# Attention decode with 8 KV heads: head 6's softmax placed before a loop, c and x on another queue, fewer pieces of wo and w2

## The chip, the cores and the metric

The kernel runs on one core of a Trainium2 chip. A core has engines that run their own instruction queues: PE (TensorE, matrix multiplication; PEld is its weight load), DVE (VectorE), ACT (ScalarE), POOL (GpSimd) and SP (SyncE, which here only issues DMAs). Sixteen DMA engines move data between HBM and the on-chip memories (SBUF for data, PSUM for matmul results). The metric is the device time of one execution in microseconds, lower is better.

## The reference

One token (`x`, 512 numbers) goes through an adaptive-layernorm block: attention over a cache of 32,768 keys and values with 32 query heads that share 8 KV heads of 128 numbers, and a feed-forward layer with ReLU. Cut to what matters:

```python
mod = (_silu(c) @ w_mod).reshape(c.shape[0], 6, 1, -1)
sa, ca, ga, sb, cb, gb = (mod[:, i] for i in range(6))
h = _layernorm(x) * (1 + ca) + sa
# A: q = h @ wq (32 heads), scores = q k / sqrt(128), softmax over 32768, o = p v, then o @ wo
x = x + ga * A(h, k_cache, v_cache, wq, wo)
h = _layernorm(x) * (1 + cb) + sb
x = x + gb * (relu(h @ w1) @ w2)
```

Each of K and V is 8 x 32768 x 128 in bf16, 64 MiB, so nearly all of the 149.43 MB that the kernel reads is K and V.

## The kernel before

**The stream of loads.** All large inputs come through SyncE's DMA queue in one order, written out as a list (lines 139 to 144): w_mod, wq, K of head 0 in two halves, then for each head the halves of K of the next head and V of this one in turn, then V of head 7 in three pieces, wo in four (WOP, line 47: heads 0 to 3, 4 and 5, 6, 7), w1 in two, w2 in six (W2P, line 51). `need` (line 147) issues loads up to the one asked for. K and V halves, 4 MB each, go into a ring of five slots, so a load waits for the slot that an earlier one leaves. `c` and `x` come through GpSimd's queue (lines 156 and 157) into 16 rows of 64 numbers, eight rows each; lines 216 to 233 turn them into columns with a mask (`pick8`) and four matmuls.

**A head.** There are four K tiles per head, `u` = 0 to 3, each in two `half`s. `turn_k` (line 398) transposes one half of a tile in place on VectorE (line 405). `scores` (line 412) multiplies it with the queries: eight matmuls of 128x512 (line 422) into one PSUM bank for two tiles. `bank_max` (line 427) copies the bank to SBUF and takes each row's maximum on VectorE. `softmax` (line 433) is a generator; each `next` emits one part:

1. `m_p`, the maximum of the two halves (VectorE, line 437)
2. its transpose on TensorE (`mT_ps`, line 440)
3. `Mrow` and `Mexp` on VectorE (lines 443 and 448)
4. a transpose back on TensorE (`Mb_ps`, line 454), and on ScalarE the bias (line 456) and all exponentials (`P_g`, line 459)
5. the transposed probabilities `PT_g` (line 465) and `Lexp` (line 468) on VectorE
6. the sum over partitions on TensorE (`L_ps`, line 471)
7. its reciprocal on VectorE (`Linv`, line 474)

`pv` (line 477) multiplies the probabilities with two V tiles, 32 matmuls. For heads 0 to 5, and for the first half of head 6, it is a hardware loop in a section of its own (line 490): before its first matmul TensorE goes through a series of semaphore waits and sets the loop's registers. `blocks` (line 509) adds the four parts of a head's output on VectorE, `o_cols` (line 520) transposes it on TensorE, `normalise` (line 528) scales it and `spread` (line 544) brings a group of heads into the form that `project` (line 555) multiplies with wo.

**The order.** From line 599 the order of TensorE's and VectorE's instructions is the order in which the program emits them; an instruction that waits holds up all behind it on its engine. An iteration `g` of the loop at line 611 does the scores of head `h = g + 1` and V of head `g`, and spreads the softmax parts of head `g` over the first scores of head `h`. LAST is 7 and LOOPED is 6. At the end of iteration 5 comes part 1 of head 6's softmax, then the loop over V's second half of head 5, then part 2; iteration 6 begins with three `turn_k` of head 7 and emits parts 3 to 7 between its scores. The last iteration ends with V of head 6 and head 7, unrolled; then come `project`, the second layernorm, w1 and w2. `keep_clock` (line 592) emits matmuls whose result is not used.

Of the kernel before, what the change touches and what calls it, by code (L numbers as in the profile page):

```python
# [9 lines left out]
BF16 = mybir.dt.bfloat16  # L10
F32 = mybir.dt.float32
ACT = mybir.ActivationFunctionType
ALU = mybir.AluOpType
# [4 lines left out]
def kernel(  # L18
# [14 lines left out]
    nc = tc.nc  # L33
    P = 128
    _, _, D = A_x.shape
    _, Hkv, Sk, Dh = A_k_cache.shape
    Hq = A_wq.shape[1] // Dh
    REP = Hq // Hkv
# [8 lines left out]
    WOP = [(0, Hkv // 2), (Hkv // 2, Hkv // 4), (Hkv - 2, 1), (Hkv - 1, 1)]  # L47
    WOROWS = 2
    LAST = Hkv - 1
    LOOPED = Hkv - 2  # L50
    W2P = [(0, 4), (4, 7), (7, 10), (10, 12), (12, 13), (13, 14)]
    W1P = [(0, KT - 1), (KT - 1, KT)]
    assert Dh == 128 and REP == 4 and D == 512 and FT == W2P[-1][1] and NTILE == 4
    scale = float(Dh) ** -0.5
# [6 lines left out]
    vv = A_v_cache[0].rearrange("g (p j) d -> g p j d", p=P)  # L61
    wm_v = w_mod.rearrange("(p kt) n -> p kt n", p=P)
    wq_v = A_wq.rearrange("(p kt) n -> p kt n", p=P)
    def wo_v(i):
        g0, n = WOP[i]
        return A_wo[g0 * REP * Dh:(g0 + n) * REP * Dh, :].rearrange("(p r) d -> p r d", p=P)

    w1_v = B_w1.rearrange("(p kt) f -> p kt f", p=P)
    w2_v = B_w2.rearrange("(p f) d -> p f d", p=P)

# [4 lines left out]
    const = ctx.enter_context(tc.tile_pool(name="const", bufs=1))  # L75
# [10 lines left out]
    loaded, last_loop = {}, []  # L86
# [3 lines left out]
    def piece(name, at, n):  # L90

        if name not in pieces:
            pieces[name] = ring.tile([P, 2 * TK * Dh], BF16, tag="slot", name=name)
        return pieces[name][:, at:at + n]

    def load(key):
        kind = key[0]
        if kind == "wm":
            t = ring.tile([P, KT, 6 * D], BF16, tag="slot", name="wm_sb")
            src = wm_v  # L100
        elif kind == "wq":
            t = ring.tile([P, KT, Hq * Dh], BF16, tag="slot", name="wq_sb")
            src = wq_v
        elif kind in "kv":
            g, steps = key[1], key[2]
            src = (kv if kind == "k" else vv)[g, :, TK * steps[0]:TK * (steps[-1] + 1), :]
            name = "Ksb" if kind == "k" else "Vsb"
            if len(steps) == 2:
                t = ring.tile([P, TK * len(steps), Dh], BF16, tag="slot", name=name)
            else:  # L110
                t = piece(name, TK * Dh * (steps[0] % 2), TK * Dh).rearrange("p (j d) -> p j d", d=Dh)
        elif kind == "wo":
            g0, n = WOP[key[1]]
            t = piece("wo_sb", g0 * REP * D, n * REP * D).rearrange("p (r d) -> p r d", d=D)
            src = wo_v(key[1])
        elif kind == "w1":
            k0, k1 = W1P[key[1]]
            t = piece("w12_sb", k0 * Dff, (k1 - k0) * Dff).rearrange("p (kt f) -> p kt f", f=Dff)
            src = w1_v[:, k0:k1]
        else:  # L120
            f0, f1 = W2P[key[1]]
            t = piece("w12_sb", KT * Dff + f0 * D, (f1 - f0) * D).rearrange("p (f d) -> p f d", d=D)
            src = w2_v[:, f0:f1]
        stream_dma(t[:], src)
        if kind in "kv":
            for i, u in enumerate(steps):
                loaded[(kind, g, u)] = t[:, TK * i:TK * (i + 1), :]
        else:
            loaded[key] = t[:]

    def stream_dma(dst, src):
        i = nc.sync.dma_start(out=dst, in_=src)
        tc.stamp_issue_order_token(i.ins, "sp_stream")
        if last_loop:

            tc.add_manual_dep(i.ins, last_loop[0], mybir.DependencyInfo(
                mybir.DependencyClass.NoSync, mybir.DependencyReason.DATA))

    stream = [("wm",), ("wq",)] + [("k", 0, (2 * G, 2 * G + 1)) for G in range(NG)]
    for g in range(LAST):  # L140
        for G in range(NG):
            stream += [(kind, gg, (2 * G, 2 * G + 1)) for kind, gg in (("k", g + 1), ("v", g))]
    stream += [("v", LAST, (0, 1)), ("v", LAST, (2,)), ("v", LAST, (3,))] + [("wo", i) for i in range(len(WOP))]
    stream += [("w1", i) for i in range(len(W1P))] + [("w2", i) for i in range(len(W2P))]
    pos = [0]

# [5 lines left out]


    wm_sb = need(("wm",))
    cx_row = const.tile([16, D // 8], BF16)
    nc.gpsimd.dma_start(out=cx_row[0:8], in_=c[0].rearrange("(a n) -> a n", a=8))
    nc.gpsimd.dma_start(out=cx_row[8:16], in_=A_x[0, 0].rearrange("(a n) -> a n", a=8))

    ident_bf = const.tile([P, P], BF16)
    make_identity(nc, ident_bf[:])  # L160
# [8 lines left out]
    for hp in range(4):  # L169
        h, par = hp // 2, hp % 2  # L170
        src = AP(ib.tensor, ib.offset + 64 * h + par, [[ib.ap[0][0], P], [0, 4], [2, 32]])
# [8 lines left out]
        out=mask4, in_=ident_f[:].rearrange("p (x q) -> p q x", q=REP), op=ALU.add, axis=AX.X,  # L180
# [3 lines left out]
    for n in sorted({n * REP for _, n in WOP}):  # L184
# [28 lines left out]
    hid_bd = const.tile([P, FT, KT, KT], BF16)  # L213
    nc.gpsimd.memset(hid_bd[:], 0.0)

    pick8 = const.tile([16, 8], BF16)
    nc.vector.tensor_tensor(out=pick8[:], in0=ident_bf[0:16, 0:8], in1=ident_bf[0:16, 8:16], op=ALU.add)
    cx_sel = const.tile([16, 2], BF16)
    nc.vector.tensor_copy(out=cx_sel[:], in_=cmask[8][0:16, 0:2])
    cx_bd = const.tile([16, 8, D // 8], BF16)  # L220
    nc.vector.tensor_tensor(  # L221
        out=cx_bd[:], in0=cx_row[:].unsqueeze(1).to_broadcast([16, 8, D // 8]),
        in1=pick8[:].unsqueeze(2).to_broadcast([16, 8, D // 8]), op=ALU.mult,
    )
    xc_ps = small_ps([P, KT, 2], "xc_ps")
    for kt in range(KT):
# [171 lines left out]
    def turn_k(g, u, half):  # L398

        if u == 0 and half == 0:  # L400
            S_tiles[g] = spool.tile([P, NG, 512], F32, tag="S_g", name="S_g")
            m_tiles[g] = spool.tile([P, NG], F32, tag="m2", name="m2")
        Ksb = need(("k", g, u))
        KTt = Ksb[:, 32 * half:32 * half + 32, :].rearrange("p j d -> p (j d)")
        t = nc.vector.transpose(out=KTt.bitcast(F32), in_=KTt.bitcast(F32))  # L405
        KT_tiles[g, u, half] = KTt
        if loop:

            tc.add_manual_dep(t.ins, loop.pop(), mybir.DependencyInfo(
                mybir.DependencyClass.NoSync, mybir.DependencyReason.DATA))  # L410

    def scores(g, u, half):

        t4 = (2 * u + half) % 4
        if t4 == 0:
            S_ps_tiles[g] = bank("S_ps")
        KTv = KT_tiles.pop((g, u, half)).rearrange("p (jj h i par) -> p jj h i par", jj=32, h=2, i=32, par=2)
        for sl in range(2):
            s = 2 * t4 + sl
            for hp in range(4):  # L420
                h, par = hp // 2, hp % 2
                nc.tensor.matmul(  # L422
                    S_ps_tiles[g], lhsT=qbd[g % 2][:, hp, 4 * (7 - s):4 * (7 - s) + P], rhs=KTv[:, 16 * sl:16 * sl + 16, h, :, par],
                    start=(t4 == 0 and sl == 0 and hp == 0), stop=(t4 == 3 and sl == 1 and hp == 3),
                )
# [94 lines left out]
    def o_cols(g):  # L520
        nc.tensor.matmul(  # L521
            oT_ps, lhsT=Y_tiles.pop(g)[:], rhs=qsel, start=True, stop=True, skip_group_check=True,
        )
# [75 lines left out]
    with tc.manual_schedule(engines={mybir.EngineType.PE, mybir.EngineType.DVE}):  # L599
# [11 lines left out]
        for g in range(LAST):  # L611
            h = g + 1
            build_qbd(h)
            turn_k(h, 0, 0)
            turn_k(h, 0, 1)
            turn_k(h, 1, 0)
            scores(h, 0, 0)
            if soft:
                next(soft)
            open_o(g)  # L620
            scores(h, 0, 1)
            if soft:
                next(soft)
            if g > 0:
                blocks(g - 1)
            scores(h, 1, 0)
            if g > 0:
                o_cols(g - 1)
            turn_k(h, 1, 1)
            scores(h, 1, 1)  # L630
            if soft:
                next(soft)
            if g > 0:
                normalise(g - 1)
                if g in [sum(w) for w in WOP]:
                    spread(part_of(g - 1))
            if soft:
                next(soft)
            bank_max(h, 0)
            next(soft or iter(()), None)  # L640
            pv(g, (0, 1))
            for u in (2, 3):
                for half in range(2):
                    turn_k(h, u, half)
                    scores(h, u, half)
            bank_max(h, 1)
            soft = softmax(h)
            next(soft)
            if g < LOOPED:
                pv(g, (2, 3))  # L650
                next(soft)
                continue
            next(soft)
            next(soft)
            pv(g, (2,), range(6))
            next(soft)
            next(soft)
            open_o(LAST)
            pv(g, (2,), range(6, 16))
            pv(g, (3,))  # L660
            next(soft)
            next(soft, None)
            a_rows.append(row_bank("a_ps"))
            blocks(g)
# [109 lines left out]
```

## Time and profile before

| | before |
|---|---|
| median of 3 runs | 355.39 us (355.18 to 355.49) |
| the profiled execution's own time | 355.74 us |
| its span, from the first to the last instruction | 353.9 us |
| PE busy | 279.8 us (79%) |
| DVE busy | 203.1 us (57%) |
| ACT busy | 25.4 us (7%) |
| read from HBM | 149.42 MB, 422 GB/s over the span |
| mean granted TensorE clock | 0.947 |

The profile gives every instruction of one execution with its start, its length and what released it from a wait; times are counted from the first instruction. "L422" is line 422 of the kernel. In the page's slices the span is cut into 40 equal parts, and a digit is a share in tenths. A timeline row has the start, the duration, the engine, the line, the operation, output `<-` inputs, how many instructions were merged, and in brackets how long the engine stood idle before it and what ended that. A row of a table by stretches has, for each engine, busy microseconds and the number of instructions, then the granted clock of TensorE (1.00 is full), the busy share of the DMA engines and the rate.

### The profile page before, as it was taken

What the parts mean: (1) busy time and instruction counts of PE and PEld (TensorE: products, weight loads), DVE (VectorE), ACT (ScalarE), POOL (GpSimd) and SP (SyncE); (2) the same over time, 40 slices, a digit from 0 to 9 for tenths busy, and PEclk for the clock granted to TensorE, in tenths of its full rate; (3) what the DMA queues carried; (4) which work ended last, traced back from release to release, by engine and by line L of the source; (5) the groups of instructions that cost most, each with busy time, mean ns of one, the idle gap of its engine ahead of it and who ended that gap; (6) DMA issues with size and microseconds to landing.
All of it is one profiled execution on the core that took longest, in us unless ns stands there. A gap on an engine that the chain in (4) does not pass through costs nothing. (4 is left out here: it accounts for less than half of the span.)

```text
span 353.9 us, 4006 instructions
## 1 busy us (share of the span) xinstructions
PE 279.8 (79%) x1311; PEld 112.7 (32%) x1311; DVE 203.1 (57%) x271; ACT 25.4 (7%) x69; POOL 3.9 (1%) x16
## 2 busy tenths in 40 slices
PE   0542781999898979897979796979689687989996
PEld 0221230333343323332323232323234233334444
DVE  6245775882768268462939178553938095734142
ACT  1220003000010001000100001000100010002000
POOL 4000000000000000000000000000000000000000
PEclk9995997799899999998999899999999997999999
DMA  8999999999999999999999999999999999999994
GB/s 309 455 422 445 431 422 441 441 418 424 459 418 422 459 418 424 441 437 426 433 444 417 430 456 419 427 446 426 422 448 430 422 439 441 422 430 424 421 420 177
DMA packets 6852, 149.59 MB, mean 423 GB/s; under 512 B 824, under 2 KB 1080, under 8 KB 1976
## 3 DMA queue, kind: packets, MB, share of 16 engines
q1 hardware_dynamic: 6776, 149.43, 98.4%
q8 instruction: 8, 0.13, 0.1%
q14 instruction: 4, 0.03, 0.0%
q0 software_dynamic: 64, 0.00, 0.0%
HBM read 149.42 MB, written 0.00 MB: 422 GB/s over the span
## 5 line engine op out<-in xcount | busy, mean ns | idle before, releaser
L405 DVE STREAM_TRANSPOSE Ksb<-Ksb 128x2048 f32<-128x2048 f32 x64 | 142.9, 2281 | 63.9 <-DMA Ksb<-in_A_k_cache_dram 63.9
L484 PE MATMUL o_ps<-Vsb,PT_g 128*16 (+1 forms) x512 | 130.0, 395 | 21.5 <-ACT qbd L389 7.2
L422 PE MATMUL S_ps<-Ksb,qbd 128*128 128x512 bf16 x512 | 121.8, 388 | 23.5 <-DVE Ksb L405 21.9
L422 PEld LDWEIGHTS <-qbd 128*128 128x128 bf16 x512 | 49.0, 98 | 87.6 <-issue 31.8
L484 PEld LDWEIGHTS o_ps<-Vsb,PT_g 128*16 x416 | 37.4, 90 | 90.2 <-issue 63.7
L428 DVE TENSOR_SCALAR_CACHE_REDUCE S_g<-S_ps 128x512 f32<-128x512 f32 x16 | 11.0, 690 | 34.4 <-PE S_ps L422 34.4
L389 ACT COPY qbd<-qrep_sb 32x16 bf16<-32x16 bf16 x32 | 6.4, 201 | 138.7 <-PE S_ps L422 137.6
L465 DVE STREAM_TRANSPOSE PT_g<-P_g 128x1024 bf16<-128x1024 bf16 x8 | 9.7, 1218 | 6.6 <-ACT P_g L459 6.6
L484 PEld LDWEIGHTS <-PT_g 128*16 128x16 bf16 x96 | 8.2, 90 | 11.0
L456 ACT ACTIVATE nbias<-Mb_ps 128x1 f32<-128x1 f32 x8 | 1.4, 171 | 136.8 <-PE Mb_ps L454 136.8
L459 ACT ACTIVATE P_g<-S_g,nbias 128x1024 bf16<-128x1024 f32 x8 | 9.2, 1148 | 0.2
L227 PE MATMUL xc_ps<-cx_sel,cx_bd 16*128 16x2 bf16 x4 | 0.3, 172 | 11.1 <-DVE cx_bd L221 11.1
L515 DVE SCALAR_TENSOR_TENSOR Y<-o_ps,smask,Y 16x128 f32<-16x128 f32 x24 | 8.1, 339 | 0.8
L471 PE MATMUL L_ps<-Lexp,ones_f 128*128 128x4 f32 x16 | 3.0, 257 | 4.3 <-DVE Lexp L468 4.3
L597 PE MATMUL spare_ps<-qbd,ident_bf 128*128 128x512 bf16 x19 | 5.6, 380 | 0.0
L440 PE MATMUL mT_ps<-ident_f,m_p 128*1 128x128 f32 x8 | 2.2, 270 | 3.9 <-DVE m_p L437 2.0
L471 PEld LDWEIGHTS L_ps<-Lexp,ones_f 128*128 128x128 f32 x16 | 3.1, 221 | 5.8 <-issue 5.1
L443 DVE TENSOR_REDUCE Mrow<-mT_ps 1x4 f32<-1x128 f32 x8 | 2.1, 257 | 4.6 <-PE mT_ps L440 4.6
L534 DVE TENSOR_TENSOR oT_sb<-acc_ps,Linv 128x4 bf16<-128x4 f32 x8 | 1.2, 150 | 5.7 <-PE acc_ps L521 5.7
L295 PE MATMUL mod_ps<-wm_sb,siluT 128*1 128x512 bf16 x24 | 3.6, 624 | 1.0 <-DVE siluT L289 1.0
L505 DVE MEMSET o_ps<- 16x512 f32 x8 | 3.9, 485 | 0.8
L552 DVE CAST o_sb<-o_ps 128x4 bf16<-128x4 f32 (+2 forms) x4 | 0.7, 167 | 5.7 <-PE o_ps L548 5.7
(115 smaller groups left out, 80.0 us busy)
## 6 DMA issues: line engine op xcount, KB each, us to landing
Ksb<-in_A_k_cache_dram SPq DMA_DIRECT2D x16, 4096.0 KB, 35.6
Vsb<-in_A_v_cache_dram SPq DMA_DIRECT2D x15, 4096.0 KB, 35.2
wq_sb<-in_A_wq_dram SPq DMA_DIRECT2D x1, 4096.0 KB, 19.6
Vsb<-in_A_v_cache_dram SPq DMA_DIRECT2D x2, 2048.0 KB, 31.8
wm_sb<-in_w_mod_dram SPq DMA_DIRECT2D x1, 3072.0 KB, 10.4
wo_sb<-in_A_wo_dram SPq DMA_DIRECT2D x1, 2048.0 KB, 29.1
w_sb<-in_B_w_dram SPq DMA_DIRECT2D x1, 1344.0 KB
wo_sb<-in_A_wo_dram SPq DMA_DIRECT2D x1, 1024.0 KB, 31.1
```

Source lines behind the costliest of these rows:

```text
L295: nc.tensor.matmul(dst[j // 4][32 * (j % 4):32 * (j % 4) + 1, :], lhsT=src_T[:, kt:kt + 1], rhs=w[:, kt, j * 512:(j + 1) * 512], start=(kt ...
L389: nc.scalar.copy(out=o, in_=i)
L405: t = nc.vector.transpose(out=KTt.bitcast(F32), in_=KTt.bitcast(F32))
L422: nc.tensor.matmul(S_ps_tiles[g], lhsT=qbd[g % 2][:, hp, 4 * (7 - s):4 * (7 - s) + P], rhs=KTv[:, 16 * sl:16 * sl + 16, h, :, par], start= ...
L428: nc.vector.tensor_scalar(out=S_tiles[g][:, G, :], in0=S_ps_tiles[g], scalar1=1.0, scalar2=None, op0=ALU.mult, op1=ALU.max, accum_out=m_ti ...
L459: nc.scalar.activation(out=P_g[:], in_=S_g[:].rearrange("p g f -> p (g f)"), func=ACT.Exp, bias=nbias[:], scale=scale, accum_out=l_g[:],)
L465: nc.vector.transpose(out=PT_g[:], in_=P_g[:])
L471: nc.tensor.matmul(L_ps[:], lhsT=ones_f[:], rhs=Lexp[:], start=True, stop=True)
L484: nc.tensor.matmul(o_tiles[g][:], lhsT=PT, rhs=Vx, start=False, stop=False, skip_group_check=True)
L505: nc.vector.memset(o_tiles[g][:], 0.0)
L515: nc.vector.scalar_tensor_tensor(out=Y[:], in0=o[:, s], scalar=smask[:, s:s + 1], in1=Y[:], op0=ALU.mult, op1=ALU.add,)
L597: nc.tensor.matmul(spare[0], lhsT=ident_bf[:], rhs=qbd[0][:, :, 0:P], start=True, stop=True)
```

## The change

It has four parts.

- `c` and `x` are loaded through SyncE's queue, behind w_mod and ahead of wq, into 32 rows of 32 numbers, sixteen rows each. The masks that turn them into columns follow (`pick16`, `cmask[16]`); the number of matmuls stays at four.
- wo's third and fourth piece (heads 6 and 7) are one DMA; `project(2)` and `project(3)` read parts of the same load.
- w2 comes in five pieces, of 5, 4, 3, 1 and 1 of its 14 columns of tiles, where it came in six of 4, 3, 3, 2, 1 and 1.
- At the end of iteration 5, parts 2, 3 and 4 of head 6's softmax are emitted ahead of the loop over the second half of head 5's V. In iteration 6 all four `turn_k` of head 7's first two tiles come first, parts 5, 6 and 7 follow the first, second and fourth block of scores, and `o_cols` of head 5 comes behind the fourth block.

```diff
-    W2P = [(0, 4), (4, 7), (7, 10), (10, 12), (12, 13), (13, 14)]
+    W2P = [(0, 5), (5, 9), (9, 12), (12, 13), (13, 14)]
...
         elif kind == "wo":
-            g0, n = WOP[key[1]]
-            t = piece("wo_sb", g0 * REP * D, n * REP * D).rearrange("p (r d) -> p r d", d=D)
-            src = wo_v(key[1])
+            parts = key[1]
+            (g0, n), m = WOP[parts[0]], len(parts)
+            t = piece("wo_sb", g0 * REP * D, m * n * REP * D).rearrange("p (g x) -> p g x", g=m)
+            src = A_wo[g0 * REP * Dh:(g0 + m * n) * REP * Dh, :].rearrange("(g p r) d -> p g (r d)", g=m, p=P)
...
-    stream += [("v", LAST, (0, 1)), ("v", LAST, (2,)), ("v", LAST, (3,))] + [("wo", i) for i in range(len(WOP))]
+    stream += [("v", LAST, (0, 1)), ("v", LAST, (2,)), ("v", LAST, (3,))] + [("wo", parts) for parts in ((0,), (1,), (2, 3))]
...
-    cx_row = const.tile([16, D // 8], BF16)
-    nc.gpsimd.dma_start(out=cx_row[0:8], in_=c[0].rearrange("(a n) -> a n", a=8))
-    nc.gpsimd.dma_start(out=cx_row[8:16], in_=A_x[0, 0].rearrange("(a n) -> a n", a=8))
+    cx_row = const.tile([32, D // 16], BF16)
+    for i, src in enumerate((c[0], A_x[0, 0])):
+        stream_dma(cx_row[16 * i:16 * i + 16], src.rearrange("(a n) -> a n", a=16))
...
             turn_k(h, 0, 0)
             turn_k(h, 0, 1)
             turn_k(h, 1, 0)
+            if h == LAST:
+                turn_k(h, 1, 1)
             scores(h, 0, 0)
...
             scores(h, 1, 0)
-            if g > 0:
+            if h < LAST:
+                if g > 0:
+                    o_cols(g - 1)
+                turn_k(h, 1, 1)
+            scores(h, 1, 1)
+            if h == LAST:
                 o_cols(g - 1)
-            turn_k(h, 1, 1)
-            scores(h, 1, 1)
             if soft:
-                next(soft)
+                next(soft, None)
...
             next(soft)
+            if g == LOOPED - 1:
+                next(soft)
+                next(soft)
+                next(soft)
             if g < LOOPED:
                 pv(g, (2, 3))
-                next(soft)
+                if g < LOOPED - 1:
+                    next(soft)
                 continue
```

More of the change, by code (lines that the diff above doesn't have):

```diff
@@ L63 @@
     wq_v = A_wq.rearrange("(p kt) n -> p kt n", p=P)
-    def wo_v(i):
-        g0, n = WOP[i]
-        return A_wo[g0 * REP * Dh:(g0 + n) * REP * Dh, :].rearrange("(p r) d -> p r d", p=P)
     w1_v = B_w1.rearrange("(p kt) f -> p kt f", p=P)
@@ L127, in load @@
                 loaded[(kind, g, u)] = t[:, TK * i:TK * (i + 1), :]
+        elif kind == "wo":
+            for m, i in enumerate(parts):
+                loaded[("wo", i)] = t[:, m].rearrange("p (r d) -> p r d", d=D)
         else:
@@ L214 @@
     nc.gpsimd.memset(hid_bd[:], 0.0)
[L216 to L220, printed above, removed]
+    pick16 = const.tile([32, 16], BF16)
+    nc.vector.tensor_tensor(out=pick16[:], in0=ident_bf[0:32, 0:16], in1=ident_bf[0:32, 16:32], op=ALU.add)
+    cx_sel = const.tile([32, 2], BF16)
+    nc.vector.tensor_copy(out=cx_sel[:], in_=cmask[16][0:32, 0:2])
+    cx_bd = const.tile([32, 16, D // 16], BF16)
     nc.vector.tensor_tensor(
-        out=cx_bd[:], in0=cx_row[:].unsqueeze(1).to_broadcast([16, 8, D // 8]),
-        in1=pick8[:].unsqueeze(2).to_broadcast([16, 8, D // 8]), op=ALU.mult,
+        out=cx_bd[:], in0=cx_row[:].unsqueeze(1).to_broadcast([32, 16, D // 16]),
+        in1=pick16[:].unsqueeze(2).to_broadcast([32, 16, D // 16]), op=ALU.mult,
     )
@@ L637 @@
             if soft:
-                next(soft)
+                next(soft, None)
             bank_max(h, 0)
@@ L648 @@
             next(soft)
+            if g == LOOPED - 1:
+                next(soft)
+                next(soft)
+                next(soft)
             if g < LOOPED:
                 pv(g, (2, 3))
-                next(soft)
+                if g < LOOPED - 1:
+                    next(soft)
                 continue
```

## The prediction

> **What bounds the kernel now.** I read the page first, then the chain, then the engines' timelines around the loop that the change touches, last the SyncE queue at the end. The page's slices:
>
> ```profile
> span 353.9 us, 4006 instructions
> PEclk9995997799899999998999899999999997999999
> DMA  8999999999999999999999999999999999999994
> PE 11%; DVE 1%; issue 0%; ACT 0%; ACTq 0%
> ```
>
> The DMA engines are busy in every slice up to the last, so the stream of 149.43 MB is one limit. The other is the chain, nearly all PE, which reaches back only to 307.74 us. Behind that the timeline shows TensorE without a gap worth naming: scores of head 7's last blocks from 307.78, head 6's and 7's V halves, the projections, the FFN, whose last matmul starts at 351.0. Which of the two ends last? SyncE's queue, at the end:
>
> ```profile
> 340.52 0.33 SPq L132 DMA_DIRECT2D w_sb<-in_B_w_dram  x1
> 341.81 0.33 SPq L132 DMA_DIRECT2D w_sb<-in_B_w_dram  x1
> SPq L132 <- DMA wo_sb<-in_A_wo_dram: 8.4, 4, 4.5
> ```
>
> These two issues are w2's last pieces. They were held until wo's third and fourth piece had landed, so their start times are also those landings. From issue to landing w2's pieces took at least 8.7 us (the line's own figures, 8.7/12.4/23.8): 341.81 + 8.7 = 350.5 for the last one. Its four matmuls need about 0.3 us (56 take 3.29 us, plus the tail of one): 350.85 at the earliest, against 351.2 in this execution. TensorE's chain is 0.35 us late, and no speed-up of it brings more than that.
>
> Where does the chain's lateness come from? TensorE and then VectorE, in the stretch that the change rewrites:
>
> ```profile
> 276.87 1.02 PE L484 MATMUL o_ps<-Vsb,PT_g 128*16 x4 [1.82 <-issue]
> ...
> 286.63 0.27 PE L440 MATMUL mT_ps<-ident_f,m_p 128*1 128x128 f32 x1 [0.34 <-PEq L490]
> 286.74 3.64 PE L422 MATMUL S_ps<-Ksb,qbd 128*128 128x512 bf16 x16
> 290.67 0.22 PE L454 MATMUL Mb_ps<-ident_f,Mexp 1*128 1x1 f32 x1 [0.30 <-DVE Mexp L448]
> ...
> 294.78 2.77 PE L422 MATMUL S_ps<-Ksb,qbd 128*128 128x512 bf16 x8 [1.73 <-DVE Ksb L405]
> ```
> ```profile
> 283.51 6.70 DVE L405 STREAM_TRANSPOSE Ksb<-Ksb 128x2048 f32<-128x2048 f32 x3 [7.53 <-DMA Ksb<-in_A_k_cache_dram]
> 290.13 0.23 DVE L443 TENSOR_REDUCE Mrow<-mT_ps 1x4 f32<-1x128 f32 x1
> ...
> 292.44 2.29 DVE L405 STREAM_TRANSPOSE Ksb<-Ksb 128x2048 f32<-128x2048 f32 x1
> 294.66 1.19 DVE L465 STREAM_TRANSPOSE PT_g<-P_g 128x1024 bf16<-128x1024 bf16 x1
> 295.79 0.18 DVE L468 TENSOR_SCALAR Lexp<-mask_sb,l_g 128x4 f32<-128x4 f32 x1
> ```
>
> K of head 7 lands at 283.5 and VectorE is then full. Its fourth transpose of K stands behind Mrow, Mexp, a memset and the four of `blocks`, 2.3 us, and the last scores wait for it. They take 2.77 us where the same eight took 1.90 at 256.08 and 217.44: the clock.
>
> ```profile
> core 0: us, PE busy (x) PEld busy (x) DVE busy (x) ACT busy (x) POOL busy (x), PEclk, DMA share, GB/s
> 159.10:162.50 3.40, 1.49 (x7) 0.43 (x5) 0.86 (x3) 0.81 (x4) 0.00 (x0) 1.00 0.94 405
> 275.16:278.57 3.41, 1.55 (x7) 0.67 (x8) 0.78 (x3) 0.00 (x0) 0.00 (x0) 1.00 0.93 404
> 292.22:295.64 3.42, 1.69 (x9) 0.79 (x8) 3.42 (x3) 0.15 (x2) 0.00 (x0) 1.00 0.91 393
> 295.64:299.05 3.41, 2.75 (x10) 1.31 (x9) 1.48 (x8) 0.00 (x0) 0.00 (x0) 0.50 0.98 423
> ```
>
> Each stretch is 3.41 us. Where TensorE was busy 1.49 or 1.69 us, the next one has clock 0.50; after 1.55 at 275.16 it stayed 1.00. About half busy is the edge. Here the half clock lasted from 295.64 to 302.46 and cost 0.9 us in the scores and 0.9 in the loop from 298.65 (8.94 us against 8.01 at 220.41). A run without it has 1.8 us of slack on TensorE, is ended by the DMA stream and reads 0.35 us less: 355.74 - 0.35 = 355.39, the median of the runs. That may be chance, since profiling can add something of its own.
>
> **c and x.** Two issues go from GpSimd (0.65 and 0.52 us, at 1.25 and 1.89), whose masks start about 1.1 us sooner; two of about 0.4 join SyncE's queue behind w_mod, so wq's issue moves from 1.20 to some 2.1. The engines are on w_mod until it lands (SyncE waits for that until about 11.1), which hides it. The rows now come behind w_mod: about 11.2 instead of 10.2 (1.89 + 8.3). cx_bd, silu, mod and q follow 1.0 us later; qbd is ready at 26.80 + 1.0, and head 0's scores start at 32.84, with K's transpose. So 0; with that cover gone it would be +1.0. V's first load (17.13) shifts by as much, behind three K loads and wq, 16 MB, some 38 us of queue. What GpSimd's queue costs the stream isn't shown (its 64 packets are 0.0%); bounds: a gain of 0.6 us, a loss of 0.1; I take 0, by the packets' share.
>
> **w2 in five, wo's last two in one.** The same bytes, two DMAs fewer, 128 row packets fewer of 6852: 0 to -0.1 us at the end of the stream, I take -0.05. Each new w2 piece lands at the time of its old last row; the first matmul at 347.89 needs 5/14 of w2, estimated to be there at 347.7 (350.5 less 9/14 of 1.84 MB at 422 GB/s), and the other pieces keep ahead in the same way: 0. But `project(2)` used wo's third piece alone. Its first weights load at 341.42, and the joint piece is there at 341.81: up to 0.4 us of new wait on PE, with all the FFN behind it.
>
> **Softmax of head 6 ahead of the loop.** mT, Mrow, Mexp, Mb leave the stretch after the loop and come before it, one waiting for the other while PE stands: from m_p's end at 275.97, 0.27 + 0.28 + 0.21 + 0.22 with four handovers of 0.04 end at 277.14. From a last weight load to the loop's first one takes 1.23 us (219.18 to 220.41), so the loop starts at 278.15 instead of 276.84: +1.3. The old entry followed VectorE's m_p by 0.87; should the new one wait for ScalarE's exponentials too (0.17 + 1.15 + 0.19), it is 279.4, +2.5. The nearest row is the first; the other bounds it. Queued behind are the whole loop and head 7's first scores: they start at about 288.0 to 289.2 instead of 286.74. SyncE's next V load waits for that loop (286.45), with 35 us from issue to landing before it: 0.
>
> **Head 7's blocks.** VectorE now does four transposes in a row, 8.89 us (as the four from 302.99): 283.51 to 292.40, 2.3 us sooner. Then PT_g and Lexp, 1.31 us from 294.66 to 295.97 in the old rows: 293.63. L_ps now stands on PE between the second and third block of scores and must wait for it, to 293.7; PE has come there by 291.6 to 292.9, so the cover for the late loop is 0.8 to 2.1 us. Behind L_ps: sixteen score matmuls (0.31 later, 3.64 long, to 297.65), o_cols (0.38; it had been done in the gap at 292.67), normalise on VectorE (0.40), spread at 298.45, entry 1.23: the loop starts at **299.68 instead of 298.65**. At full clock 8.01 us: it ends at 307.69, against 307.59. So 2.3 us won on VectorE are given away by putting L_ps and o_cols into the line; the net is +0.1 against the profiled execution and +1.9 against one without its half clock.
>
> **Sum.** +0.1 at the loop's end; then `project(2)` would be ready at 341.52 and waits to 341.81 + 0.05: +0.43; less 0.05: about +0.4. 355.74 + 0.4 = **356.1**, 0.7 over the median, 0.2%. About 0.2% is what a measurement of this kernel can tell from no change.
>
> **Rivals.**
> The *half clock in the new gap*: if the loop starts at 278.15 and runs at full clock, PE stands from 291.6 to 293.7; a stretch that holds 1.8 us of it leaves the next at 0.50, just when sixteen matmuls in a row are the chain: 3.41/2 = +1.7, no longer covered by anything, 357.5 in all. Against it: the waits ahead of the loop (2.6 us idle of 3.1) would often take the clock there instead, which fills the later gap. It decides from a gap of about 1.8 us. The stretches' phase differs from run to run: 18%.
> The Trainium skill, TensorE: Matmul & The Clock Gate, "Part 1: The HAM clock gate", has the clock fall after an idle window of about 3.4 us and warns of idle gaps longer than that. By that rule no gap here would be long enough and this rival falls to 0; the rows above speak against it, for 292.22 to 295.64 was half busy, its longest gap 1.73 us.
> *The end stays with the DMA*: if the entry is 0.5 us quicker than 1.23 and wo lands in time, the chain passes at 350.85 and the time is 355.3 (355.0 to 355.5), the change invisible: 22%.
> *The stream gets shorter*: without GpSimd's packets, all 0.6 us of the bound and a chain that follows, 354.6: 8%. Against it speaks the loop's start at 299.7.
> The forecast, 355.7 to 356.4, has 52%, half of it beyond 0.2%. So faster 8%, same 22 + 26 = 48%, slower 18 + 26 = 44%. The range is 354.9 to 357.6; it leaves out the 8% and some of the half-clock case.
>
> **What would show it.** Right: the loop on V5's last half starts after 278; L_ps waits for Lexp near 293.7; the loop on V6's first half starts near 299.7 and takes 8.0; a gap before line 567's first weights. Wrong: that loop starts before 299, or takes 9; a clock of 0.50 behind 293; w2's last issue or landing far from 350.5.

## The result, and the profile after

The changed kernel takes **356.36 us** (median of 22 runs, 355.55 to 359.69), beside 355.27 us (22 runs, 354.96 to 355.49) for the kernel before in the same measurement. The ratio is 1.0044, with a 95% interval of 1.0028 to 1.006: a little slower, and its runs are far more scattered. They stand in groups: eight runs at 355.55 to 355.81 us, seven at 356.13 to 356.61, three at 357.15 to 357.82, and four at 359.18 to 359.69. The mean granted clock of TensorE is 0.947 to 0.956 in the first group, 0.937 to 0.942 in the second, 0.942 to 0.947 in the third and 0.928 to 0.933 in the last: lowest where the time is longest, though it doesn't fall from group to group.

The profiled execution took 356.51 us. From its page, the span, the granted clock and the DMA engines in 40 slices:

```profile
span 354.7 us, 3994 instructions
...
PEclk9995997699899999998999898999999898999999
DMA  8999999999999999999999999999999999999993
```

The span is 0.8 us longer than before. The clock dips (8) in slice 32, at 275 to 284 us, and in slice 34, at 293 to 301; before there was one dip in this stretch, in slice 34. The DMA engines have less to do in the last slice than before (3 tenths, before 4), so the stream ended sooner beside the end of the span: TensorE is what came last. TensorE's timeline, from the loop over the second half of head 5's V to the end:

```profile
278.30 8.89 PE L484 MATMUL o_ps<-Vsb,PT_g 128*16 x32 [1.23 <-issue]
287.38 3.64 PE L422 MATMUL S_ps<-Ksb,qbd 128*128 128x512 bf16 x16 [0.19 <-PEq L490]
293.70 0.36 PE L471 MATMUL L_ps<-Lexp,ones_f 128*128 128x4 f32 x2 [2.68 <-DVE Lexp L468]
293.92 3.64 PE L422 MATMUL S_ps<-Ksb,qbd 128*128 128x512 bf16 x16
297.49 0.38 PE L521 MATMUL acc_ps<-mask_sb,Y 16*128 16x4 f32 x2
298.39 0.18 PE L548 MATMUL o_ps<-rsel,oA 128*128 128x8 bf16 x1 [0.52 <-DVE oA L535]
299.70 8.76 PE L484 MATMUL o_ps<-Vsb,PT_g 128*16 x32 [1.13 <-DVE S_g L428]
308.64 7.12 PE L422 MATMUL S_ps<-Ksb,qbd 128*128 128x512 bf16 x32 [0.19 <-PEq L490]
...
342.51 0.67 PE L567 MATMUL acc_ps<-o_sb,wo_sb 128*128 128x1 bf16 x16
...
348.78 3.29 PE L745 MATMUL ffn_ps<-w_sb,hid_bd 128*4 128x128 bf16 x56
```

The wait before the last scores is gone and another stands between the second and the third block: 2.68 us in which TensorE waits for `Lexp`, with `L_ps` behind it. The loop over the first half of head 6's V (line 484 at 299.70) ends at 308.46, where it ended at 307.59 before, and from there everything is later by as much: the FFN starts at 348.78 instead of 347.89, 0.89 us, and the execution is 0.77 us longer. No wait for wo can be seen ahead of line 567. In the kernel before, the same loop of head 4, at full clock, and then this one:

```profile
220.41 8.01 PE L484 MATMUL o_ps<-Vsb,PT_g 128*16 x32 [0.84 <-DVE Linv L474]
298.65 8.94 PE L484 MATMUL o_ps<-Vsb,PT_g 128*16 x32 [0.66 <-PE L_ps L471]
```

VectorE in the same stretch of the changed kernel:

```profile
283.43 8.89 DVE L405 STREAM_TRANSPOSE Ksb<-Ksb 128x2048 f32<-128x2048 f32 x4 [6.63 <-DMA Ksb<-in_A_k_cache_dram]
292.24 1.20 DVE L465 STREAM_TRANSPOSE PT_g<-P_g 128x1024 bf16<-128x1024 bf16 x1
293.37 0.19 DVE L468 TENSOR_SCALAR Lexp<-mask_sb,l_g 128x4 f32<-128x4 f32 x1
...
297.90 0.16 DVE L534 TENSOR_TENSOR oT_sb<-acc_ps,Linv 128x4 bf16<-128x4 f32 x1 [2.38 <-PE acc_ps L521]
```

VectorE is through with K's four transposes at 292.32 and gives out `Lexp` at 293.56; TensorE has been idle since 291.02. The table by stretches shows what this does to the clock:

```profile
279.26:282.68 3.42, 3.37 (x9) 1.10 (x9) 0.00 (x0) 0.00 (x0) 0.00 (x0) 0.50 1.04 450
...
289.50:292.92 3.42, 1.52 (x7) 0.48 (x5) 3.42 (x3) 0.00 (x0) 0.00 (x0) 1.00 0.93 402
292.92:296.33 3.41, 2.63 (x14) 1.31 (x15) 2.40 (x8) 0.00 (x0) 0.00 (x0) 1.00 1.00 432
296.33:299.74 3.41, 1.76 (x10) 0.81 (x8) 1.16 (x5) 0.00 (x0) 0.00 (x0) 1.00 1.07 456
299.74:303.15 3.41, 3.41 (x9) 1.17 (x10) 0.38 (x1) 0.00 (x0) 0.00 (x0) 0.50 1.05 452
303.15:306.57 3.42, 3.42 (x18) 1.41 (x17) 3.42 (x2) 0.00 (x0) 0.00 (x0) 1.00 0.98 422
```

The stretch with the wait for `L_ps` (289.50, TensorE busy 1.52 us) left the clock alone. The next gap, behind the fourth block, where TensorE does `o_cols`, waits for VectorE's `normalise`, spreads and enters the loop, took it (296.33, busy 1.76 us): the loop's first 3.41 us ran at half clock, 9 matmuls in a stretch against 18 in the next. The loop took 8.76 us where 8.01 was forecast: 0.75 us. (The loop before took 8.94, at half clock too, and began 1.05 us sooner.) The first row is the loop over head 5's V, part of which ran at half clock behind the softmax's waits; `L_ps` comes behind it and waits for VectorE, so this cost the chain nothing.

### The profile page after: what moved, and what is told of

Its sections match the earlier page's. It is cut to its first block, busy times and chain, and to the rows that moved or that the text cites. A ratio compares the mean times of both kernels' runs of the same rounds, so it can differ in the third digit from the quotient of the medians.

```text
span 354.7 us, 3994 instructions
## 1 busy us (share of the span) xinstructions
PE 280.6 (79%) x1311; PEld 112.9 (32%) x1311; DVE 202.6 (57%) x271; ACT 25.4 (7%) x69; POOL 2.7 (1%) x14
```

## Theories

- **The clock in the new gaps** (mine after the result): with `L_ps` and `o_cols` in TensorE's line there are two gaps that the old order did not have, and the half clock behind either is on the chain. Where the stretches of 3.41 us, for which the clock is granted, begin differs from run to run, hence the groups.
- **Length alone**: the waits cost what they last, the clock is a side show.
- **The loads**: wo's joint piece, w2's larger pieces or c and x end the execution later, and the order is harmless.

The experiments ran in three groups, each on a chip of its own, beside the kernel before: 355.32 us (31 runs) beside the two halves, L_ps behind and the filled gaps; 355.37 us (33 runs) beside the single loads and the order with old loads; 355.34 us (18 runs) beside the longer gap, the changed kernel again and c and x on the best order.

## Experiments: the two halves of the change

**Loads alone.** The changed kernel's loads with the old order:

```diff
-            if h == LAST:
-                turn_k(h, 1, 1)
...
-            if g == LOOPED - 1:
-                next(soft)
-                next(soft)
-                next(soft)
```

> The three changes to the loads alone (c and x on SyncE's queue, wo's last two pieces joined, w2 in five), with the order of before. If the new order is the whole cause, this is before's time, 355.1 to 355.4, with before's small spread, and the loop on V6's first half starts as before (about 298 to 298.7). If the loads carry the loss (the joint wo piece, or the later c and x), it is 355.8 to 356.4, with a gap before the first weights of line 567.

355.63 us (355.43 to 356.99, 11 runs), ratio 1.0014 (1.0004 to 1.0024). That is between the two expectations: the loads alone cost some 0.3 us. Its profile, of a run of 356.00 us, has no wait for wo ahead of line 567: its loop over the first half of head 6's V took 9.41 us at half clock, so the chain came later than the joint piece.

**Order alone.** The changed kernel's order with the old loads:

```diff
-    W2P = [(0, 5), (5, 9), (9, 12), (12, 13), (13, 14)]
+    W2P = [(0, 4), (4, 7), (7, 10), (10, 12), (12, 13), (13, 14)]
...
-    for i, src in enumerate((c[0], A_x[0, 0])):
-        stream_dma(cx_row[16 * i:16 * i + 16], src.rearrange("(a n) -> a n", a=16))
+    nc.gpsimd.dma_start(out=cx_row[0:8], in_=c[0].rearrange("(a n) -> a n", a=8))
+    nc.gpsimd.dma_start(out=cx_row[8:16], in_=A_x[0, 0].rearrange("(a n) -> a n", a=8))
```

> The new order alone, with before's loads. If the order is the whole cause: the changed kernel's times, median 356.0 to 356.7 and single runs up to 359, L_ps near 293.7 and the loop start near 299.7. If the loads carry the loss: 355.2 to 355.5.

356.09 us (355.59 to 356.38, 11 runs), ratio 1.0017 (1.0008 to 1.0026). Its trace has the two gaps too (2.03 us ahead of `L_ps`), the loop over the first half of head 6's V from 299.58 with 8.63 us, and a half clock from 299.37:

```profile
295.96:299.37 3.41, 1.87 (x10) 0.78 (x8) 1.16 (x5) 0.00 (x0) 0.00 (x0) 1.00 1.03 437
299.37:302.79 3.42, 3.21 (x8) 1.14 (x9) 0.07 (x1) 0.00 (x0) 0.00 (x0) 0.50 0.91 393
```

So both halves cost something. By the medians the order costs more (0.8 us) than the loads (0.3), but the two intervals overlap. The groups at 357 to 359.7 us did not appear here in 11 runs.

## Experiments: the gap ahead of L_ps

**L_ps behind the fourth block.** The changed kernel, with part 6 of head 6's softmax moved behind the fourth block of scores and `o_cols`, so that TensorE has no reason to wait between the blocks:

```diff
-            if soft:
+            if soft and h < LAST:
                 next(soft, None)
...
             if h == LAST:
                 o_cols(g - 1)
+                next(soft)
```

> The changed kernel, with L_ps behind head 7's fourth block of scores and o_cols where it stood behind the third. If it is the place of L_ps in TensorE's line that costs, the four blocks run without a stop from 287.4 to about 294.4, the loop starts at 296.5 to 297.5 and the time is that of the DMA stream's end: 355.0 to 355.3, with a small spread. If moving the softmax ahead of the loop costs by itself (the later loop on V5), it stays at 355.8 or above.

355.64 us (355.41 to 357.04, 12 runs), ratio 1.0012 (1.0003 to 1.0022). Its timeline on TensorE:

```profile
279.48 9.01 PE L484 MATMUL o_ps<-Vsb,PT_g 128*16 x32 [1.21 <-ACT nbias L456]
288.68 7.12 PE L422 MATMUL S_ps<-Ksb,qbd 128*128 128x512 bf16 x32 [0.19 <-PEq L490]
...
298.41 8.04 PE L484 MATMUL o_ps<-Vsb,PT_g 128*16 x32 [1.22 <-DVE S_g L428]
...
341.40 0.69 PE L567 MATMUL acc_ps<-o_sb,wo_sb 128*128 128x1 bf16 x16 [0.73 <-DMA wo_sb<-in_A_wo_dram]
```

The 32 score matmuls run without a stop, and although the loop ahead of them began 1.2 us later than in the changed kernel, the next loop starts 1.3 us sooner (298.41; 296.5 to 297.5 was expected) and at full clock. The gain of 2.0 us at that loop's end (306.45 against 308.46) is then cut short: `project(2)` waits 0.73 us for wo's joint piece, which the changed kernel's late chain never met. The time goes to that of the loads alone (355.63), not to the 355.0 to 355.3 expected. So the order's cost in the changed kernel comes from `L_ps` at its place, and it is nearly all gone without it. Two of the 12 runs lie at 357.0 us. Runs at 356.8 to 357.2 came only in kernels with wo's joint piece (the loads alone, the joint piece alone, the changed kernel and kernels made from it); the joint piece's own trace, below, shows one way to such a time.

**Filling the gaps.** The changed kernel with matmuls whose result is not used: ten in the gap ahead of `L_ps`, two behind `o_cols`, two behind the spread.

```diff
+            if h == LAST:
+                fill(10)
...
                 o_cols(g - 1)
+                fill(2)
...
+            if h == LAST:
+                fill(2)
             pv(g, (0, 1))
```

> The changed kernel with 14 matmuls more whose results nobody uses: ten of 128x512 ahead of L_ps, two behind o_cols, two ahead of the loop. They add no work to the chain where it waits anyway. If the spread of the changed kernel (355.55 to 359.69) is TensorE's clock falling after these gaps, all runs lie at 355.5 to 356.0 and the granted clock is 1.00 from 290 to 315. If the gaps cost by their length alone, median and spread stay (356.4, up to 359).

356.16 us (356.12 to 356.81, 7 runs), ratio 1.0027 (1.0016 to 1.0038). On TensorE:

```profile
290.72 2.32 PE L606 MATMUL fill_ps<-qbd,ident_bf 128*128 128x512 bf16 x10
293.51 0.36 PE L471 MATMUL L_ps<-Lexp,ones_f 128*128 128x4 f32 x2 [0.47 <-DVE Lexp L468]
...
300.03 8.04 PE L484 MATMUL o_ps<-Vsb,PT_g 128*16 x32 [1.21 <-DVE S_g L428]
```

The waits end as before; only the clock is kept, at 1.00 from there on. The loop starts 0.33 us later, by the fill ahead of it, and still ends sooner (308.07 against 308.46). Six of the seven runs lie within 0.35 us, and none is above 356.81, where the changed kernel's runs spread over 4.1 us. That speaks for the clock as the cause of the groups, though seven runs are few: the order alone had no long run in 11. The times themselves are above the 355.5 to 356.0 expected. With the clock at full, 356.16 less the 0.33 of the fill is about 355.8 (an estimate), where the changed kernel's first group lies, 0.5 us over the kernel before: the part that is length alone. Length alone can't give the rest.

**A longer gap.** The changed kernel with head 6's `PT_g` transposed twice, so that `Lexp` comes later. (The second one writes the same tile, where the expectation speaks of a tile of its own.)

```diff
-        nc.vector.transpose(out=PT_g[:], in_=P_g[:])
+        for _ in range(2 if g == LOOPED else 1):
+            nc.vector.transpose(out=PT_g[:], in_=P_g[:])
```

> The changed kernel with head 6's PT_g transposed a second time into a tile of its own ahead of Lexp's chain, so that the gap in which TensorE waits for L_ps grows by about 1.2 us (from 2.7 to 3.9 us). Theory that the granted clock falls when too few matmul columns stream in a window of 3.41 us: it now falls in every run, the 16 scores of the fourth block take 0.427 us each for at least one window, and the time is 358.0 to 360 us. Rival, that the gap costs its length and no more: 355.75 + 1.2 = 356.9 to 357.2 us.

359.32 us (356.98 to 361.3, 6 runs), ratio 1.0104 (1.0074 to 1.0134). On TensorE:

```profile
295.07 0.36 PE L472 MATMUL L_ps<-Lexp,ones_f 128*128 128x4 f32 x2 [4.11 <-DVE Lexp L469]
295.29 5.31 PE L422 MATMUL S_ps<-Ksb,qbd 128*128 128x512 bf16 x16
...
302.89 8.63 PE L485 MATMUL o_ps<-Vsb,PT_g 128*16 x32 [1.28 <-DMA Ksb<-in_A_k_cache_dram]
```

`L_ps` comes 1.4 us later and the time is 2.7 us longer than the changed kernel's on the same chip (356.62, next): twice the length. The sixteen score matmuls take 5.31 us instead of 3.64. Length alone, 356.9 to 357.2 us, holds for one run of six (356.98). That the clock "falls in every run" was too much: a gap of 4.1 us that the border of two stretches cuts in half leaves 3.41 - 2.05 = 1.36 us of matmuls in each, at the upper end of the edge found below (an estimate).

**The changed kernel again**, unaltered.

> The changed kernel again, unaltered, beside the two others on the same chip. Both theories: a median of 356.1 to 356.7 us. Theory of the clock's windows: its runs fall into groups, from 355.5 us (no window at half clock on the chain) to 359.7 us, lower granted clocks with the longer times; rival, that the long runs belonged to the chip of the first measurement: none here above 357.3 us.

356.62 us (356.45 to 358.11, 6 runs), ratio 1.0033 (1.0021 to 1.0045). The profile caught the run of 358.11 us:

```profile
293.58 0.35 PE L471 MATMUL L_ps<-Lexp,ones_f 128*128 128x4 f32 x2 [2.89 <-DVE Lexp L468]
293.80 5.32 PE L422 MATMUL S_ps<-Ksb,qbd 128*128 128x512 bf16 x16
...
301.25 8.76 PE L484 MATMUL o_ps<-Vsb,PT_g 128*16 x32 [1.13 <-DMA Ksb<-in_A_k_cache_dram]
```

The wait ends at the same time as in the first profile (293.58, there 293.70), but now the clock falls behind it as well: the scores take 5.32 instead of 3.64 us and the loop 8.76 instead of 8.01, 1.68 + 0.75 us. The first profile, with the second drop alone, read 356.51 us; this one reads 1.6 more. So the same program gives 356.5 or 358.1 by whether one of the two gaps loses the clock or both. A run above 357.3 us on a second chip also speaks against the rival that the long runs belonged to the first. No trace was caught of a run of the first group, and no run here was under 356.4: that both gaps keep the clock there is the theory's account, and not shown. The group at 359.2 to 359.7 us stays open: 355.8 with both drops, 1.68 + 0.75, gives 358.2, a full 1 us less (an estimate). Its lower granted clock fits more half clock somewhere; where, no trace shows.

## Experiments: the loads

**c and x alone.** The old kernel with `c` and `x` in SyncE's queue, sixteen rows each, and nothing else of the change.

```diff
-    cx_row = const.tile([16, D // 8], BF16)
-    nc.gpsimd.dma_start(out=cx_row[0:8], in_=c[0].rearrange("(a n) -> a n", a=8))
-    nc.gpsimd.dma_start(out=cx_row[8:16], in_=A_x[0, 0].rearrange("(a n) -> a n", a=8))
+    cx_row = const.tile([32, D // 16], BF16)
+    for i, src in enumerate((c[0], A_x[0, 0])):
+        stream_dma(cx_row[16 * i:16 * i + 16], src.rearrange("(a n) -> a n", a=16))
```

> Before with c and x on SyncE's queue alone. The three load changes together gave 355.43 to 356.99, median 0.3 us over before, which the prediction had put at nothing beside an early chain. If c and x cause the runs near 357 (the stream as a whole starts or ends later in some runs), this has runs above 356 too. If they are hidden as predicted: 355.1 to 355.8, as before.

355.75 us (355.53 to 356.2, 11 runs), ratio 1.0012 (1.0003 to 1.0021): some 0.4 us in the medians that I had at nothing.

**The same edit where the DMA ends last.** This adds it to the kernel of "L_ps behind, old loads" below:

```diff
-    nc.gpsimd.dma_start(out=cx_row[0:8], in_=c[0].rearrange("(a n) -> a n", a=8))
...
+        stream_dma(cx_row[16 * i:16 * i + 16], src.rearrange("(a n) -> a n", a=16))
```

> The order with L_ps behind the fourth block and the old loads of wo and w2 (355.41 us, DMA end as the floor), with one edit: c and x in SyncE's queue, sixteen rows each. Theory that this edit moves the end of the DMA stream: the floor itself moves, 355.6 to 355.8 us, as the edit alone gave on the old order (355.75). Rival, that it only delays the first scores and so acts through the chain, which in this order is ahead of the DMA: 355.1 to 355.5 us, as without the edit.

355.57 us (355.25 to 355.96, 11 runs), ratio 1.0005 (0.9996 to 1.0013). It lies between the two expectations and decides nothing: 0.16 us over the kernel without the edit, which ran on another chip, and not to be told from the kernel before. By the two medians the edit costs 0.2 to 0.4 us; by this interval it may cost nothing.

**wo's joint piece alone.** The old kernel with this edit, and with the lines in `load` that read a joint piece, as in the change:

```diff
...
-    stream += [("v", LAST, (0, 1)), ("v", LAST, (2,)), ("v", LAST, (3,))] + [("wo", i) for i in range(len(WOP))]
+    stream += [("v", LAST, (0, 1)), ("v", LAST, (2,)), ("v", LAST, (3,))] + [("wo", parts) for parts in ((0,), (1,), (2, 3))]
```

> Before with wo's last two pieces joined, alone. If the joint piece sets the chain's earliest pass (project for head 6 can't start before the last of wo is there, near 341.5), the fastest runs move up to 355.4 to 355.5 and the median to 355.5 to 355.7. If it is hidden: 355.1 to 355.4 as before.

355.71 us (355.51 to 356.99, 11 runs), ratio 1.0008 (0.9999 to 1.0017): near what was expected if the joint piece sets the chain's earliest pass, but hardly to be told from the kernel before. The profile caught the run of 356.99 us, the one far from the rest. Timeline and stretches of its tail:

```profile
341.58 0.70 PE L567 MATMUL acc_ps<-o_sb,wo_sb 128*128 128x1 bf16 x16 [1.07 <-DMA wo_sb<-in_A_wo_dram]
...
343.59 1.15 PE L597 MATMUL spare_ps<-qbd,ident_bf 128*128 128x512 bf16 x3
...
347.27 0.93 PE L714 MATMUL hid_ps<-w_sb,h2T 128*1 128x448 bf16 x16
```
```profile
340.50:343.92 3.42, 2.35 (x46) 1.73 (x46) 0.53 (x2) 0.00 (x0) 0.00 (x0) 1.00 1.00 422
343.92:347.33 3.41, 3.41 (x15) 0.84 (x16) 1.80 (x13) 0.29 (x1) 0.00 (x0) 0.50 1.01 401
347.33:350.74 3.41, 3.28 (x50) 2.09 (x50) 0.71 (x2) 0.50 (x2) 0.00 (x0) 1.00 0.53 198
```

An early chain (this run's loop over V had kept the full clock) stands 1.07 us for the joint piece, and the gap takes the clock in the second layernorm: from line 567 to w1's product it is 5.69 us (341.58 to 347.27), against 4.46 in the changed kernel's profile (342.51 to 346.97). The busy time of 340.50 is 2.35 us, and the clock fell all the same: many of its 46 matmuls stream one column.

**w2 in five alone.** The old kernel with this one edit:

```diff
-    W2P = [(0, 4), (4, 7), (7, 10), (10, 12), (12, 13), (13, 14)]
+    W2P = [(0, 5), (5, 9), (9, 12), (12, 13), (13, 14)]
```

> Before with w2 in five pieces alone. The last piece is the same, so the end of the stream and the time are before's, 355.1 to 355.5; if the larger early pieces hold up the last matmuls, 355.5 or more, with a gap inside the 56.

355.62 us (355.44 to 355.99, 11 runs), ratio 1.0008 (0.9999 to 1.0017), again hardly to be told from the kernel before. The FFN in its timeline:

```profile
347.42 3.43 PE L735 MATMUL ffn_ps<-w_sb,hid_bd 128*4 128x128 bf16 x56 [0.31 <-ACT hid_bd L725]
```

The 56 matmuls took 3.43 us instead of 3.29: where the second and the third piece begin, a matmul starts 0.15 and 0.12 us after the one before it, and 0.055 is the rule. The piece of three tiles lands late, at 349.54 by the trace, and 20 matmuls stand behind it. They end 0.69 us after the last landing (350.16).

**L_ps behind, old loads.** The order of "L_ps behind the fourth block" with all the old loads; its edits are those of that kernel and of "order alone":

```diff
-    W2P = [(0, 5), (5, 9), (9, 12), (12, 13), (13, 14)]
+    W2P = [(0, 4), (4, 7), (7, 10), (10, 12), (12, 13), (13, 14)]
...
-            if soft:
+            if soft and h < LAST:
                 next(soft, None)
```

> The new order with L_ps behind the fourth block, and before's loads. With the joint wo piece the early chain stood 0.73 us at line 567 for wo. If that wait held the third experiment at 355.4 to 355.8, this passes it and ends with the DMA stream: 355.0 to 355.3 with no run above 355.6, at best 0.1 us under before. If something else held it, 355.4 to 355.8 again.

355.41 us (355.08 to 356.04, 11 runs), ratio 1.0001 (0.9992 to 1.001). From its page, the chain that ended last, by engine:

```profile
DMA 12%; PE 0%; DVE 0%; issue 0%
```

and the end of TensorE's timeline:

```profile
347.51 3.52 PE L746 MATMUL ffn_ps<-w_sb,hid_bd 128*4 128x128 bf16 x56 [0.22 <-DMA w_sb<-in_B_w_dram]
```

Now the FFN waits for w2, and the end is the DMA stream's: the last landing at 350.59, the last matmul's end 0.44 us later. This is the best order tried. Its loop over the first half of head 6's V starts at 298.24, about 1.5 us ahead of the changed kernel's, and yet it is not faster than the kernel before; 355.0 to 355.3 and no run above 355.6 had been expected. So 355.3 to 355.4 us is the floor that the stream sets.

## Why the prediction was right or wrong

The time was near where the prediction put it, 356.36 us for 356.1, but the sum got there by a wrong pair of terms. Between the medians it is 1.09 us, where 0.7 was forecast. Of the prediction's own signs of being right three came (the starts after 278, near 293.7 and near 299.7) and two did not (a loop of 8.0 us, a gap before line 567); of its signs of being wrong the clock of 0.50 behind 293 came.

- **What bounds the kernel: right.** That TensorE's chain is only 0.35 us behind the DMA stream, and that no speed-up of it brings more, is what the last kernel shows: an order with the chain ahead gives 355.41 us, beside 355.37 for the kernel before, and a chain that ends with the DMA.
- **Softmax ahead of the loop: right.** The loop starts at 278.30 (278.15 was worked out, 279.4 the bound; the terms ahead of it add up to 277.11, not 277.14, and the last of them ended at 277.08). The entry took the nearest row's 1.23 us, so the bound was not needed. The loop behind it was sized by one row: it took 8.89 us where the old profile had 9.41 (276.87 to 286.28), so the scores started at 287.38, ahead of the 288.0 to 289.2 worked out, and the gap ahead of `L_ps` was 2.68 us, more than the 0.8 to 2.1 of the forecast. As `L_ps` waits for VectorE, that moved nothing behind it.
- **Head 7's blocks: right, up to the loop's start.** `L_ps` at 293.70 (293.7), the next loop at 299.70 (299.68): 2.3 us won on VectorE and given away in TensorE's line. Taking `L_ps` out of that place brought 2.0 us back at the loop's end.
- **"At full clock 8.01 us: it ends at 307.69": the step that failed.** The loop took 8.76 us and ended at 308.46, and +0.1 was +0.87. This term, put at full clock, was short by 0.75 us. I looked for the half clock in the gap ahead of `L_ps` alone and made it a rival with 18%; the gap behind the fourth block, which the same edit creates by putting `o_cols`, `normalise`, spread and the loop's entry behind each other, I had priced at its length. In all three profiles of this order with its two gaps untouched (two of the changed kernel, one of the order alone) the clock fell in that second gap; in one it fell in both. 14 of the 22 runs lie above 356.1 us.
- **"About half busy is the edge": wrong.** Busy 1.52 us kept the clock, 1.76 and even 2.35 lost it. What sorts these three is the time in which columns stream: 1.36, 1.13 and 1.05 us (last section). The Trainium skill, TensorE: Matmul & The Clock Gate, "Part 1: The HAM clock gate", lets the clock fall after an idle window of about 3.4 us; the drop at 295.14 us behind a gap of 2.89 us (the changed kernel again), and the lost loop time with no gap above 1.3 us, disagree with it, so I was right not to go by it. Its account of a window that runs free fits the traces: the stretches began at another point in each.
- **The price of the rival: right in size.** 1.7 us was worked out for the half clock in the first gap; 1.68 was measured in the scores. The argument against it failed: the clock did fall in the waits ahead of head 5's loop, as in every profile of a new order, yet that didn't fill the gap. What decided was the phase. The stretch with the wait for `L_ps` streamed 1.36 us in the first profile and kept the clock; in the second it streamed 1.35 and lost it.
- **wo's joint piece: the mechanism right, its place in this sum wrong.** The wait is there whenever the chain is early (0.73 and 1.07 us), to 341.40 and 341.58 where 341.81 + 0.05 was forecast. In the changed kernel the chain comes at 342.5, later than the piece, and the wait was 0. The sum's +0.43 was +0.1 at the loop's end and +0.33 of this wait; in the profiled execution they were +0.87 and 0, and the median agrees partly by luck.
- **"The other pieces keep ahead in the same way: 0": wrong at the floor.** With the chain early, w2 in five made the 56 matmuls 0.14 us longer (3.43 for 3.29, one profile). In the changed kernel's own profile the FFN never waits (3.29 us), so it is hidden there.
- **c and x at 0: the cover held, the 0 is open.** The rows came at 11.75 us (11.2 was worked out), head 0's scores at 33.01 instead of 32.84 us: hidden, as said. Yet the edit alone reads 1.0012 (1.0003 to 1.0021). The profiles can't show where the 0.4 us lies: the one of the edit caught a run of 355.53 us, faster than the profiled one of the kernel before (355.74), with w2's last landing at 350.23 beside 350.52 and the time outside the span the same (1.78 and 1.80 us). A gain of 0.6 us, for which no row was given, did not come; the loss may be larger than the 0.1. What the loss is stays open.
- **The costs don't add.** c and x, wo and w2 alone read 0.2 to 0.4 us each in the medians, and all three together 0.3. A likely reason, which no run separates, is that wo and w2 each hold back a chain that would else have met the same floor, so that one wait hides behind the other.

## What to carry to other kernels

When an order written out by hand moves an instruction that waits, look at every gap that the new order leaves on TensorE up to the next long block of matmuls, and count the columns that stream in each 3.4 us around it: a gap of 2 us can cost its length and the block's first 3.4 us at half speed. An engine that is freed 2.3 us sooner brings nothing while the transfers end at the same time; find that floor first, and judge an edit of the chain and an edit of the loads each against it. And a change whose runs fall into groups needs more than three runs, and more than one profile, since one profile shows one phase.

## What the hardware showed

The granted clock changes on a grid of 3.413 us, and the grid starts at another point in each run. I counted, in 13 profiles (before, after and the eleven experiments), for each stretch of the grid that lies between 100 and 340 us, the time in which the matmuls' columns streamed. A matmul's busy time in the profile also has its latency, so 512 columns were taken as 0.217 us, the median distance between the starts of the score matmuls at full clock, and as twice that at half clock. A float32 column was counted four times; counted once, it moves no edge by more than 0.02 us.

After full-clock stretches with up to 1.27 us the clock fell to 0.50 each time, 41 of 41; from 1.36 us up it stayed each time, 806 of 806; between, at 1.32 to 1.35 us, it fell twice and stayed twice. At half clock it came back after stretches of 2.36 us or more (43 of 43) and stayed low up to 2.29 us (7 of 7); ahead of 100 us one with 2.53 us stayed low too, so this edge is less sharp. So in these traces the edge for falling is at 37 to 40% of a stretch, about six matmuls of 512 columns, and for coming back at some 70%. The second edge fits the old kernel's profile, in which the half clock lasted two stretches, from 295.64 on: 2.15 us streamed in the first.
